# Attention pairs of the second and third batches in groups of two, and the first pass's units on four PSUM banks

## The chip, the cores and the metric

The kernel runs on one core of one Trainium2 chip. The metric is device time in microseconds of one execution. Five engines work side by side, each on its own queue, in order: PE (TensorE), DVE (VectorE), ACT (ScalarE), POOL (GpSimd) and SP, which issues the DMAs. An instruction that waits for a semaphore holds up all that stands behind it on its engine.

## What is computed

Attention over 8 batches, 8 heads, 576 positions and 64 channels, with a local mask on four heads (a window of 32) and a strided mask on the other four (every 32nd position), and then a feed-forward layer of 2048 channels on the result:

```python
def _attn_ref(q, k, v):
    scores = scale * np.matmul(q, k.transpose(0, 1, 3, 2))
    rel = pos[:, None] - pos[None, :]
    mask_local = (rel >= 0) & (rel < stride)
    mask_strided = (rel >= 0) & (pos[None, :] % stride == pos[:, None] % stride)
    ...
    attn = np.exp(scores - np.max(scores, axis=-1, keepdims=True))
    attn = attn / (np.sum(attn, axis=-1, keepdims=True) + 1e-09)
    return np.matmul(attn, v)

def _moe_ref(x, w_in, w_out):
    h = x @ w_in
    g = h * (1.0 / (1.0 + np.exp(-1.702 * h)))
    return (g @ w_out)
```

x holds the attention's result, 4608 tokens by 512 channels.

## The kernel before

**Passes and slots.** The first layer (x times w_in) is done batch by batch, in passes. Pass 0 (the first batch) is 64 plain *units* of six matmuls of 128x288 each, eight for each of the eight slices n of the weights (`unit`, `plain`). Every later pass is 56 *products* of six such matmuls, seven for each slice (`product`), whose seven results `combine` adds up on ACT and DVE. Every operand is a high and a low part; the six matmuls are high by high, high by low and low by high, over two chunks. One unit or product is one *slot* of a hand-written order: the main loop (the last lines of the listing) issues the matmuls of slot s and then, with `sided(s)`, whatever was registered for that slot with `side(s, f, ...)`, in the order of registration. All five engines keep this program order. Pass 0 runs to slot 60 (its last three units lie among the next pass's products), pass 1 is slots 61 to 116, pass 2 slots 117 to 172, and so on. Slots 0 to 7 are issued inside the opening, a list of steps written out by hand.

**Attention beside it.** While pass b runs, the attention of batch b+1 is done in its slots. A batch is six *pairs*, three local (l) and three strided (s). A pair goes through `scores` (32 or 48 small matmuls on PE), `masked` and `maxima` (DVE), `below` (POOL, subtracts the maximum), `exps` (ACT), `totals` (DVE, a sum and a reciprocal), `scaled` (POOL), `turn` (four transposes on PE, then a copy on ACT), `values` (small matmuls on PE) and copies of the result on ACT. For the batches with b above 2 pairs go in groups of two (`groups_of`): the scores of both in one run, into the two banks `s_banks` side by side, and the values of both in one run into the two banks `v_banks` (mx of the second set, mz of the first). For the pairs of batches 1 and 2, in passes 0 and 1, a pair goes alone, one each seven slots, and its values go into `s_banks`.

**Weights beside it.** In pass 0 the raw weights of slice i are made ready every seven slots: `w_scale` and `w_low` (ACT), `w_join` (DVE), `w_high` (ACT, casts and stores a plain copy), `w_low_part` (DVE). Slice i is used from unit 8i on. In pass 1 the sums of slice i, that the products need, are made from the plain copies: `t_load` (DMA), four `t_sum` (POOL, tile `sums`), `t_high` (ACT), `t_low` (DVE), at slots 49 (i=0), 59, 65, 72, 79, 86, 93 and 100 for `t_sum`; the second product of slice i needs `t_low`. Passes 2 and later have no `t_sum`.

**Banks.** `place` gives a unit of pass 0 its PSUM bank, in turn out of the six of `six`; a unit pair of the same bank is two slots apart, and `unit_out` copies the bank out (ACT, or DVE for f=1) and stores it.

Of the kernel before, what the change touches and what calls it, by code (L numbers as in the profile page):

```python
# [19 lines left out]
B, H, S, D = 8, 8, 576, 64  # L20
# [9 lines left out]
HALF = S // 2  # L30
FP = DFF // (2 * P)
PAIRS = 6
# [24 lines left out]
def _pairs():  # L57
    out = []
    for b in range(B):
        x = [[(kind, b, U * i) for i in range(PAIRS // 2)] for kind in "ls"]  # L60
        out += x[0] + x[1] if b == 0 else [u for i in range(PAIRS // 2) for u in (x[b < 3][i], x[b > 2][i])]
    return out


# [6 lines left out]
def attn_ffn(ctx, tc, qk, vs, weights, masks, ident, out):  # L71
# [44 lines left out]
    hbuf = cut(AT_H, HALF, 6)  # L116
# [45 lines left out]
    for j in (1, 2, 3, 0, 4, 5):  # L162
# [3 lines left out]
        t = prs[j].rearrange("p (i m) -> p i m", i=4)  # L166
# [174 lines left out]
    def values(p, banks, at=0):  # L341

        kind, b, c = pairs[p]
        nq = _size(kind)[0]
        v, pt = vts[p], pts[p % 2]
        n0 = QL if kind == "l" else RES[c] * NPOS
        for g in range(2):
            for w, (q0, n, _, nk) in enumerate(windows(kind)):
                if kind == "s":
                    n = min(n0, (w + 1) * WS) - w * WS  # L350
                for u in range(U):
                    i = U * g + u
                    o = g * n0 + (q0 if kind == "l" else w * WS)
                    for j in range(2):
                        slot = j ^ u
                        rows = slice(slot * D, slot * D + nk)
                        matmul(
                            banks[u][j * D : (j + 1) * D, at + o : at + o + n],
                            lhsT=v[rows, i, w, :], rhs=pt[rows, i * nq + q0 : i * nq + q0 + n],
                            start=True, stop=True,  # L360
                        )
        return lambda u, *how: moved(p, u, banks[u][:, at : at + 2 * n0], *how)

    def moves_of(moves):
        for u in range(U):
            for move in moves:
                move(u)
# [122 lines left out]
    def place(n, u):  # L490
        r, f, kh = (UNITS if n else HALVES)[u]
        j = 4 * n + 2 * r + f
        return r, f, kh, six[3 - f if j >= 4 * FP - 2 else j % 6][:, :HALF], hbuf[j % 6]

    def unit(n, u, some=(0, 1)):

# [185 lines left out]
    def side(s, f, *a):  # L682
        sides.setdefault(s, []).append((f, a))
# [19 lines left out]
    def groups_of(b, slots):  # L703

        for g in range(3):
            q, s, then = b * PAIRS + 2 * g, slots[g] + 2 * (g > 0), slots[g + 1]
            side(s, both_scores, q)
            for i in range(2):
                s += 2 * i * (g == 0)
                side(s + i, masked, q + i, s_banks, 256 * i)  # L710
                for f, d in (
                    (maxima, 0), (below, 0), (exps, 4), (totals, 5 + (i and g > 0)),
                    (scaled, 5 + (i and g > 0)),
                ):
                    side(s + d + i, f, q + i, s_banks)
                side(then - (3 - (g > 0), 1)[i], turn, q + i, s_banks[i])
            side(then, both_values, q)

    for b in range(B):
        at = first(b)  # L720
        if b == 1:
            for t, f, k in ((-11, x_sum, 1), (-10, x_sum, 3), (-9, x_sum, 2), (-6, x_high, 1),
                            (-5, x_low, 1), (-5, x_high, 4), (-4, x_low, 4), (-3, x_high, 0),
                            (-2, x_low, 0), (-1, x_high, 2), (0, x_low, 2), (1, x_sum, 4),
                            (2, x_high, 3), (3, x_low, 3), (4, x_high, 6), (5, x_low, 6),
                            (6, x_high, 5), (7, x_low, 5)):
                side(at + t, f, k, b)
        elif b:
            c = b == 2
            side(at - 10 - c, x_sum, 1, b)  # L730
            side(at - 9 - c, x_sum, 3, b)
            for k in range(7):
                t = at + 2 * k - 6 + (k == 1)
                side(t, x_high, k, b)
                side(t + 1, x_low, k, b)
            side(at - 4, x_sum, 2, b)
            side(at, x_sum, 4, b)
        if 1 < b < B - 1:
            groups_of(b + 1, [at + t for t in (3, 16, 30, 44)])
        for i in range(PAIRS if b < 2 else 0):  # L740
            p = (b + 1) * PAIRS + i
            s = at - 3 * b + 7 * i + 2 * (not b)
            t = (4, 5, 6, 11, 12) if b and not i else (5, 6, 7, 10, 12)
            side(s, scores, p, s_banks)
            side(s, load_qk, p + 2)
            for f, d in ((masked, 0), (maxima, 1), (below, 2), (exps, t[0]), (totals, t[1]), (scaled, t[2])):
                side(s + d, f, p, s_banks)
            side(s + t[3], turn, p, s_banks[0])
            side(s + t[4], lambda p=p: moves_of([values(p, s_banks)]))
            side(s + t[4], load_v, p + 2)  # L750

    def word(f, i):
        f(raws[i])
# [338 lines left out]
```

## Time and profile before

| | |
|---|---|
| median of 3 runs | 840.16 us (840.1 to 841.67) |
| profiled execution | 840.09 us, of which the span of the trace is 838.2 us |
| granted TensorE clock | 0.999 of full speed |
| PE busy | 823.9 us, 98% of the span |
| DVE, ACT, POOL busy | 538.0, 421.0, 482.5 us |
| DMA | 164.84 MB, 197 GB/s in the mean |

A row of a timeline is a start, a length, the engine, the operation, output<-input, the shape and the count; in square brackets stands the idle time ahead of it and who ended it. Almost every instruction carries line 87, that of the helper that keeps the order, so rows are told apart by tile and shape: `xa,w` with 128x288 is a unit or a product; `s<-arena 64*32` and `64*64 64x54` are scores; `s<-ident_sb` is the transposes of a turn; `arena<-arena,nmax` is `below`, `arena<-arena,rinv` is `scaled`, `sums<-sums` is `t_sum`; `raw` and `w` are the weights. Rows that follow each other with the same tiles are merged, with their count.

### The profile page before, as it was taken

To read this page: it belongs to the slowest core of one execution; us is meant where nothing else is said; L and a number is where in the kernel's file an instruction comes from. 1 tells how busy PE (TensorE), PEld (TensorE's weight loads), DVE (VectorE), ACT (ScalarE), POOL (GpSimd) and SP (SyncE) were. 2 spreads that over 40 slices of the span, in tenths; PEclk is the share of its full clock that TensorE was granted. 3 is DMA by queue.
4 is the path that set the end of the run, shared out by engine and by line. 5 is a ranking of instruction groups with operands and counts; after the bars stand their busy time and mean duration, and the time that the engine had idled before them with its cause. 6 is when DMAs were issued, how large, how long until landed. Compare 5 with 4: busy or idle time off the path is not lost. (4 is left out here: it accounts for less than half of the span.)

```text
span 838.2 us, 23960 instructions
## 1 busy us (share of the span) xinstructions
PE 823.9 (98%) x9821; PEld 800.2 (95%) x9821; DVE 538.0 (64%) x877; ACT 421.0 (50%) x660; POOL 482.5 (58%) x512
## 2 busy tenths in 40 slices
PE   7899999999999999999999999999999999999998
PEld 5799989999999999999999999999999999999997
DVE  5666777867767668677678856666555555555553
ACT  4665634434434434334346656565555555555550
POOL 4633886333442433334436269999877777777770
PEclk9999999999999999999999999999999999999999
DMA  9898775686776776857588944444443344344421
GB/s 339 302 397 325 216 230 177 190 265 208 223 242 208 238 237 187 264 205 230 187 268 255 280 147 149 128 158 145 137 141 127 127 134 144 126 127 129 143 82 51
DMA packets 112510, 164.84 MB, mean 197 GB/s; under 512 B 9744, under 2 KB 88336, under 8 KB 111504
## 3 DMA queue, kind: packets, MB, share of 16 engines
q1 hardware_dynamic: 112400, 163.31, 60.1%
q8 instruction: 77, 1.26, 0.6%
q14 instruction: 33, 0.27, 0.1%
HBM read 104.55 MB, written 58.72 MB: 195 GB/s over the span
## 5 line engine op out<-in xcount | busy, mean ns | idle before, releaser
L87 POOL TENSOR_TENSOR arena<-arena 128x256 f32<-128x256 f32 (+1 forms) x301 | 307.1, 1033 | 154.1 <-ACT arena L87 80.5
L87 DVE TENSOR_TENSOR xa<-arena,xa 128x576 fp32r<-128x576 f32 (+3 forms) x100 | 147.6, 1478 | 97.5 <-ACT xa L87 50.1
L87 PE MATMUL my<-xa,w 128*128 128x288 f32 x1128 | 179.5, 300 | 1.4 <-DVE arena L87 1.1
L87 ACT CAST xa<-arena 128x576 fp32r<-128x576 f32 (+3 forms) x103 | 115.3, 1140 | 101.8 <-PE s L87 74.1
L87 PEld LDWEIGHTS my<-xa,w 128*128 128x128 f32 x1128 | 156.3, 188 | 4.2 <-DVE arena L87 1.6
L87 ACT COPY arena<-mx 128x288 f32<-128x288 f32 (+4 forms) x181 | 62.6, 365 | 172.8 <-PE mx L87 132.2
L87 PE MATMUL mz<-xa,w 128*128 128x288 f32 x804 | 131.1, 299 | 0.8 <-POOL xa L87 0.8
L87 PE MATMUL mx<-xa,w 128*128 128x288 f32 x804 | 129.4, 298 | 0.0
L87 DVE TENSOR_TENSOR arena<-my,arena 128x288 f32<-128x288 f32 (+1 forms) x204 | 89.0, 443 | 53.0 <-PE my L87 51.0
L87 ACT ACTIVATE arena<-arena 128x1024 f32<-128x1024 f32 (+2 forms) x120 | 105.2, 877 | 23.2 <-POOL arena L87 13.6
L87 PEld LDWEIGHTS mz<-xa,w 128*128 128x128 f32 x804 | 112.8, 188 | 2.1 <-POOL xa L87 1.0
L87 PEld LDWEIGHTS mx<-xa,w 128*128 128x128 f32 x804 | 112.8, 188 | 0.8
L87 POOL TENSOR_TENSOR arena<-arena,nmax 128x432 f32<-128x432 f32 (+1 forms) x42 | 51.1, 1217 | 94.1 <-DVE nmax L87 90.8
L87 DVE TENSOR_TENSOR arena<-mz,arena 128x288 f32<-128x288 f32 (+1 forms) x166 | 70.1, 440 | 23.9 <-PE mz L87 18.5
L87 DVE TENSOR_TENSOR ga<-arena,ga 128x1792 fp32r<-128x1792 f32 (+1 forms) x25 | 51.9, 2075 | 51.8 <-ACT ga L87 28.3
L87 POOL TENSOR_TENSOR arena<-arena,rinv 96x512 f32<-96x512 f32 (+1 forms) x48 | 48.3, 1008 | 62.3 <-DVE rinv L87 53.5
L87 PE MATMUL mx<-w_out,xa 128*128 128x256 f32 x576 | 75.6, 281 | 0.0
L87 PE MATMUL mz<-w_out,xa 128*128 128x256 f32 x576 | 75.6, 281 | 0.0
L87 PE MATMUL my<-w_out,xa 128*128 128x256 f32 x576 | 75.6, 281 | 0.0
L87 PEld LDWEIGHTS mx<-w_out,xa 128*128 128x128 f32 x576 | 71.2, 188 | 0.0
L87 PEld LDWEIGHTS my<-w_out,xa 128*128 128x128 f32 x576 | 71.2, 188 | 0.0
L87 PEld LDWEIGHTS mz<-w_out,xa 128*128 128x128 f32 x576 | 71.2, 188 | 0.0
(81 smaller groups left out, 1031.8 us busy)
## 6 DMA issues: line engine op xcount, KB each, us to landing
hid<-arena SPq DMA_DIRECT2D x256, 144.0 KB, 3.2
arena<-hid SPq DMA_DIRECT2D x144, 256.0 KB, 3.2
arena<-qk SPq DMA_DIRECT2D x23, 448.0 KB, 4.8
arena<-qk SPq DMA_DIRECT2D x21, 472.0 KB, 5.7
arena<-vs SPq DMA_DIRECT2D x23, 384.0 KB, 4.3
out<-arena SPq DMA_DIRECT2D x34, 256.0 KB, 2.8
stage<-w_out SPq DMA_DIRECT2D x16, 512.0 KB, 4.2
raw<-w_in SPq DMA_DIRECT2D x7, 1024.0 KB, 9.2
```

What stands on the lines that cost most here:

```text
L87: ins = call(*args, **kw)
```

## The change

The pairs of batches 1 and 2 go through `groups_of` too. In pass 0 the three groups stand at slots 2, 20, 34 with the last values at 47; in pass 1 they stand where later passes have theirs (at+3, +16, +30, +44). The order of a batch's pairs is l, s everywhere. Units of pass 0 from slice 1 on go round four banks (the fifth and sixth of `six` for one half of the positions, the first and second for the other), and `v_banks` are the third and fourth; the last two units' banks stay as they were.

```diff
-        out += x[0] + x[1] if b == 0 else [u for i in range(PAIRS // 2) for u in (x[b < 3][i], x[b > 2][i])]
+        out += x[0] + x[1] if b == 0 else [u for i in range(PAIRS // 2) for u in (x[0][i], x[1][i])]
...
-        return r, f, kh, six[3 - f if j >= 4 * FP - 2 else j % 6][:, :HALF], hbuf[j % 6]
+        i = 3 - f if j >= 4 * FP - 2 else (j if j < 4 else (4, 5, 0, 1)[j % 4])
+        return r, f, kh, six[i][:, :HALF], hbuf[j % 6]
...
-        if 1 < b < B - 1:
-            groups_of(b + 1, [at + t for t in (3, 16, 30, 44)])
-        for i in range(PAIRS if b < 2 else 0):
-            p = (b + 1) * PAIRS + i
-            s = at - 3 * b + 7 * i + 2 * (not b)
-            t = (4, 5, 6, 11, 12) if b and not i else (5, 6, 7, 10, 12)
-            side(s, scores, p, s_banks)
-            side(s, load_qk, p + 2)
-            for f, d in ((masked, 0), (maxima, 1), (below, 2), (exps, t[0]), (totals, t[1]), (scaled, t[2])):
-                side(s + d, f, p, s_banks)
-            side(s + t[3], turn, p, s_banks[0])
-            side(s + t[4], lambda p=p: moves_of([values(p, s_banks)]))
-            side(s + t[4], load_v, p + 2)
+        if b < B - 1:
+            groups_of(b + 1, [at + t for t in (2, 20, 34, 47)] if not b else [at + t for t in (3, 16, 30, 44)])
```

What the change does to the order shows at two places. The first is in pass 0, slots 2 to 10, where the weights of slice 2 are made ready (tile `raw_371`; `w_638` before and `w_671` after is that slice's high and low parts). On DVE before, `w_join` (the one that writes `raw_371`) follows the first pair's maxima, and `w_low_part` (the last row) stands after the second pair's maxima:

```order
L87 SCALAR_TENSOR_TENSOR arena<-s_82,masks_sb 128x4x54
L87 SCALAR_TENSOR_TENSOR arena<-s_83,masks_sb 128x4x54
L87 TENSOR_REDUCE nmax_609<-arena 128x8
L87 SCALAR_TENSOR_TENSOR raw_371<-raw_371 128x1024
L87 TENSOR_REDUCE ssum_610<-arena 128x8
L87 RECIPROCAL rinv_611<-ssum_610 128x8
L87 SCALAR_TENSOR_TENSOR arena<-s_82,masks_sb 96x4x64
L87 SCALAR_TENSOR_TENSOR arena<-s_83,masks_sb 96x4x64
L87 TENSOR_REDUCE nmax_673<-arena 96x8
L87 TENSOR_TENSOR w_638<-raw_371,w_638 128x4x256
```

The same stretch of DVE after, from the second half of the first pair's mask on:

```order
L87 SCALAR_TENSOR_TENSOR arena<-s_83,masks_sb 96x4x64
L87 TENSOR_REDUCE nmax_634<-arena 96x8
L87 SCALAR_TENSOR_TENSOR arena<-s_82,masks_sb 128x4x54
L87 SCALAR_TENSOR_TENSOR arena<-s_83,masks_sb 128x4x54
L87 TENSOR_REDUCE nmax_652<-arena 128x8
L87 TENSOR_REDUCE ssum_635<-arena 96x8
L87 RECIPROCAL rinv_636<-ssum_635 96x8
L87 SCALAR_TENSOR_TENSOR raw_371<-raw_371 128x1024
L87 TENSOR_REDUCE ssum_653<-arena 128x8
L87 RECIPROCAL rinv_654<-ssum_653 128x8
L87 TENSOR_TENSOR w_671<-raw_371,w_671 128x4x256
```

Both pairs' masks, maxima and totals now stand ahead of `w_low_part`, and the first pair's totals ahead of `w_join`. ACT's rows there, after:

```order
L87 ACTIVATE raw_371<-raw_371 128x1024 x2
L87 ACTIVATE arena<-arena 96x4x128
L87 CAST w_671<-raw_371 128x4x256
L87 ACTIVATE arena<-arena 128x4x2x54
L87 COPY arena<-my_80 128x288
```

The two rows on `arena` are the two pairs' `exps`: the second is new between `w_high` (the cast) and the copy that frees bank `my_80`.

The second place is in pass 1, on POOL, around slot 79. Before, each `below` (by `nmax`) is followed by its pair's `scaled` (by `rinv`), and the four `t_sum` of a slice stand between pairs:

```order
L87 TENSOR_TENSOR sums<-sums 128x256 x4
L87 TENSOR_TENSOR arena<-arena,nmax_1623 128x4x2x54
L87 TENSOR_TENSOR arena<-arena,rinv_1625 128x4x2x54
L87 TENSOR_TENSOR sums<-sums 128x256 x4
L87 TENSOR_TENSOR arena<-arena,nmax_1751 96x4x128
L87 TENSOR_TENSOR arena<-arena,rinv_1753 96x4x128
```

After, around the same slot:

```order
L87 TENSOR_TENSOR sums<-sums 128x256 x4
L87 TENSOR_TENSOR arena<-arena,nmax_1740 96x4x128
L87 TENSOR_TENSOR sums<-sums 128x256 x4
L87 TENSOR_TENSOR arena<-arena,nmax_1759 128x4x2x54
L87 TENSOR_TENSOR arena<-arena,rinv_1742 96x4x128
L87 TENSOR_TENSOR arena<-arena,rinv_1761 128x4x2x54
```

Four `t_sum` now stand between the two `below` of a group, ahead of both `scaled`. It is so in all three groups of pass 1.

## Rows read from the trace of the kernel before

**Rows 1.** Windows: slots 8 to 60, pass 1, pass 2; start:end, length, busy us.

```profile
33.84:90.24 56.40, 55.23 (x825) 52.10 (x823) 37.92 (x61) 36.47 (x68) 23.59 (x20) 1.00 0.91 335
90.24:149.18 58.94, 57.61 (x810) 53.95 (x809) 43.38 (x79) 26.90 (x62) 41.95 (x39) 1.00 0.65 202
149.18:204.89 55.71, 55.71 (x843) 54.06 (x841) 39.49 (x82) 23.75 (x60) 21.16 (x26) 1.00 0.71 226
```

**Rows 2.** Timeline of PE: pass 0, then the same slots of pass 2.

```profile
32.33 0.69 PE L87 MATMUL s<-arena 64*64 64x54 f32 x32
...
33.84 0.95 PE L87 MATMUL my<-xa,w 128*128 128x288 f32 x6
...
39.75 0.66 PE L87 MATMUL s<-ident_sb,arena 128*128 128x128 f32 x4 [0.94 <-POOL arena L87]
...
52.05 0.74 PE L87 MATMUL s<-arena 64*32 64x64 f32 x48
...
53.60 0.95 PE L87 MATMUL my<-xa,w 128*128 128x288 f32 x6
54.39 0.95 PE L87 MATMUL mx<-xa,w 128*128 128x288 f32 x6
...
67.41 0.74 PE L87 MATMUL s<-arena 64*32 64x64 f32 x48
...
223.90 1.35 PE L87 MATMUL s<-arena 64*32 64x64 f32 x80
...
238.74 1.35 PE L87 MATMUL s<-arena 64*32 64x64 f32 x80
```

**Rows 3.** Timeline of ACT, then of DVE, around slice 2 in pass 0.

```profile
34.39 2.23 ACT L87 ACTIVATE raw<-raw 128x1024 f32<-128x1024 f32 x2
...
37.91 1.04 ACT L87 CAST w<-raw 128x1024 fp32r<-128x1024 f32 x1 [0.84 <-DVE raw L87]
38.86 0.39 ACT L87 COPY arena<-my 128x288 f32<-128x288 f32 x1
...
36.65 1.23 DVE L87 SCALAR_TENSOR_TENSOR raw<-raw 128x1024 uint32<-128x1024 uint32 x1 [2.27 <-ACT raw L87]
...
40.08 1.21 DVE L87 TENSOR_TENSOR w<-raw,w 128x1024 fp32r<-128x1024 f32 x1
```

**Rows 4.** Timeline of POOL, DVE and PE: one group of two in pass 2.

```profile
226.99 1.04 POOL L87 TENSOR_TENSOR arena<-arena,nmax 96x512 f32<-96x512 f32 x1 [5.67 <-DVE nmax L87]
...
227.83 0.60 DVE L87 TENSOR_REDUCE nmax<-arena 128x8 f32<-128x432 f32 x1
...
228.45 1.74 PE L87 MATMUL my<-xa,w 128*128 128x288 f32 x12
...
233.19 0.49 PE L87 MATMUL s<-ident_sb,arena 96*128 96x96 f32 x4
...
234.34 0.60 PE L87 MATMUL s<-ident_sb,arena 128*128 128x128 f32 x4
```

**Rows 5.** Timeline of POOL in pass 1.

```profile
96.01 5.76 POOL L87 TENSOR_TENSOR sums<-sums 128x256 f32<-128x256 f32 x4
...
112.93 4.76 POOL L87 TENSOR_TENSOR sums<-sums 128x256 f32<-128x256 f32 x4
...
120.45 1.04 POOL L87 TENSOR_TENSOR arena<-arena,rinv 96x512 f32<-96x512 f32 x1 [1.76 <-DVE rinv L87]
121.45 4.02 POOL L87 TENSOR_TENSOR sums<-sums 128x256 f32<-128x256 f32 x4
125.43 0.92 POOL L87 TENSOR_TENSOR arena<-arena,nmax 128x432 f32<-128x432 f32 x1
127.98 0.92 POOL L87 TENSOR_TENSOR arena<-arena,rinv 128x432 f32<-128x432 f32 x1 [1.63 <-ACT w L87]
```

**Rows 6.** Timeline of DVE in pass 1: two `t_low`.

```profile
121.65 1.61 DVE L87 TENSOR_TENSOR w<-sums,w 128x1024 fp32r<-128x1024 f32 x1
...
129.38 1.21 DVE L87 TENSOR_TENSOR w<-sums,w 128x1024 fp32r<-128x1024 f32 x1
```

## What the change will do to the time

> **What bounds the kernel now.** I read the busy times by stage first. PE is busy for 55.71 of 55.71 us in pass 2, for 57.61 of 58.94 in pass 1 and for 55.23 of 56.40 in slots 8 to 60 [rows 1]. So PE sets the time throughout, its clock is at full speed in all three stretches, and there are two ways to gain: less PE time for the small matmuls, and fewer waits of PE in passes 0 and 1. Passes 1 and 2 make the same comparison for us: each has 56 slots and the attention of a batch, one pair at a time in pass 1 and in groups of two in pass 2, and pass 1 takes 58.94 - 55.71 = 3.23 us longer. The PE timeline shows why. A slot alone takes 0.79 us (54.39 - 53.60). Two lone pairs and 14 slots take 15.36 us in an undisturbed stretch of pass 0 (52.05 to 67.41); a group and 14 slots take 14.84 us in pass 2 (223.90 to 238.74) [rows 2]. So a group saves about 0.52 us of PE against two lone pairs, because PE changes less often between large and small matmuls. The rest of the difference is waits such as that of 0.94 us at the first turn of pass 0, for POOL [rows 2].
>
> **What the change takes away.** Pass 1: its groups get the same slots as those of pass 2, so without new waits it takes 55.71 us: 3.23 us less. Slots 8 to 60: 53 slots at 0.79 are 41.87; a group costs PE 14.84 - 14 x 0.79 = 3.78 us (scores, two turns, values), three are 11.34; the first group's scores lie ahead of slot 8, 1.35 and 0.1 for the change to and fro, so 1.45 less. The sum is 51.76 us against 56.40: 4.64 less. Ahead of slot 8 one run of scores of 0.69 becomes one of 1.35, so slot 8 comes 0.66 later [rows 2]. Together -3.23 - 4.64 + 0.66 = -7.2 us, if nothing new is waited for. The number of instructions stays the same on every engine; only the order moves. From pass 2 on nothing changes.
>
> **What it adds in pass 0.** The first group stands in the middle of slice 2's weights. Before, ACT did `w_scale` and `w_low` from 34.39 to 36.62, DVE `w_join` to 37.88, ACT `w_high` to 38.95, and DVE `w_low_part` to 41.29 [rows 3]; unit 16, the first to use them, had 2 us to spare. Now the chain passes through both pairs' exps and totals. ACT starts 0.66 later, so `w_low` ends at 37.28. Exps and totals of one pair take 1.63 us, from the end of a `below` (125.43 + 0.92) to the start of its `scaled` (127.98), DVE and ACT free [rows 5]; some 0.2 of it is overlap and hand-over to POOL. So totals of pair 6 end at about 38.7, `w_join` (1.23) at 39.9, `w_high` (1.04) at 41.0; then exps and totals of pair 7 to 42.4, since they stand ahead of `w_low_part` on DVE, and `w_low_part` (1.21) at 43.6. PE meanwhile has slots 8 to 15 with no small work: 33.84 + 0.66 + 8 x 0.79 = 40.8, and its third matmul, the first that needs the low weights, is due 0.26 later, at 41.1. **PE waits 2.5 us** at unit 16 (2.9 with 1.63 in full, 2.0 if the hand-overs are shorter). Behind this wait stand all of PE's units; on DVE the copy that frees bank `mz` for unit 17 stands behind `w_low_part` and comes just in time. Slice 3 has seven slots between its last step and unit 24, and later slices more, so it happens once. In the last group of pass 0 the totals of the second pair stand behind `w_join` of slice 7, which waits for ACT; its turn two hand-overs later can be late by nothing or by about what the first turn is late before, 0.94 [rows 2]. I take 0.4.
>
> Four banks instead of six: a bank is used again five slots after its last matmul, 5 x 0.79 = 3.95 us, and its copy takes 0.39 [rows 3]. I cost this at nothing; the cover is that ACT and DVE come to the copy within 3.5 us. Where they don't, at unit 16, the wait is already in the 2.5. The weights' DMAs: the DMA share is 0.91 in slots 8 to 60 [rows 1], and the same bytes would have to go in some 2 us less. Loads of raw weights run slices ahead, so I cost it at nothing too, up to 1 us at the worst, the size of the largest wait seen in this pass.
>
> **What it adds in pass 1.** Take T as the start of a group's scores, 223.90 in pass 2. There `below` of the first pair starts at T + 3.09 and ends at T + 4.13, the second's maxima end at T + 4.53, and the turns come at T + 9.29 and T + 10.44 [rows 2, 4]. In pass 1 four `t_sum` stand between the two `below`. They take 4.02 to 4.76 us in rows without much DVE work, and 5.76 where DVE works on x at the start of the pass [rows 5]. For the second and third group: T + 4.13 + 4.02 (4.76), the second `below` 0.92, exps and totals 1.63, `scaled` 0.92: the second turn may start at T + 11.6 (12.4) instead of T + 10.44. That is 1.2 to 1.9 us late; I take 1.55. The first turn needs the second `below` and `scaled` of its own, 1.04: T + 10.1 to 10.9, 0.8 to 1.6 late; this is part of the same lateness, not beside it. Behind the late exps on ACT and the late totals on DVE stand `t_high` and `t_low` of the slice that is used just after the group; I add 0.15 (0 to 0.8) for its second product. So **1.7 us for each of two groups**. In the first group the two turns stand two slots apart, so its first turn decides: T + 4.13 + 4.02 to 5.76 + 0.92 + 1.04 = T + 10.1 to 11.9 against 9.29, 0.8 to 2.6 late. `t_low` of slice 1 and the low part of x for a product also stand behind the second mask on DVE. I take **2.1**, nearer to the long end because this is the place of the 5.76 row. Another wait of the same kind, `t_low` of the group's own slice behind both maxima, ends at T + 4.53 + 1.21 to 1.61 [rows 6], 5.7 to 6.1, where the product at T + 4.55 [rows 4] needs it 0.26 after its start: 0.9 to 1.3 late. It comes earlier in the same group, so PE is late once, by the larger of the two; it adds nothing.
>
> **The sum.** -7.2 + 2.5 + 0.4 + 2 x 1.7 + 2.1 = +1.2 us. On the profiled execution's 840.09 that is 841.3; the median of the runs, 840.16, is the same within 0.1.
>
> **Rivals.** A measurement of this kernel can tell about 0.2% from no change, 1.7 us.
> *Slower: `t_sum` holds the groups for longer.* It decides once the new waits exceed 7.2 + 1.7 = 8.9 us; I have 8.4. With the long rows it is 2.9 at unit 16, 1.0 at the late turn of pass 0, 1.9 + 0.8 in each of two groups and 2.6 + 0.4 in the first: 12.3 us, +5.1, 845.2; halfway, 843.2. For it speaks that a chain through four engines seldom beats the sum of its rows; against it that the 4.02 rows are as frequent as the 4.76 ones.
> *Slower: POOL and DVE hold each other up.* Of the two `t_low` rows one took 1.21 beside the `t_sum` that took 4.76, the other 1.61 in the stretch of the `t_sum` that took 4.02 [rows 5, 6]: each is long where the other is short. In a group `t_low` now starts among the `t_sum`, in each of three groups; if it lost a whole `t_sum` there, 4.76 / 4 = 1.2 us, and PE that much with it, it would be 3.6 more, 844.9. Against it stands that the two rows differ by 0.4 only. The Trainium skill, SBUF — State Buffer, section "Who interferes with whom", says that a DVE instruction with two SBUF inputs and a GpSimd instruction that reads SBUF exclude each other, and that the one that comes second is blocked until the first is done. By that rule the loss is the whole `t_sum`, 1.2; the trace agrees in sign and shows 0.4.
> *Slower: four banks are too few.* If ACT is blocked by a DMA while a copy waits, PE stands at each of some twelve turnovers of pass 0; 0.2 us each is +2.4, 843.7. Before, no wait of PE in that pass is for a bank.
> The Trainium skill, Perfetto Trace Analysis, section "Optimization Strategy", says that a gap that recurs on the engine that should be saturated can mean too few buffers; no such gap is in the trace of before, and by it this rival would show as a gap each fourth slot.
> *Faster: the short rows hold.* With 4.02 everywhere, 1.2 in two groups, 0.8 in the first and 2.0 at unit 16, the new waits are 5.2 and the time 838.1. If neither chain reached PE, which pass 2 shows for a POOL without `t_sum`, it would be 832.9. Against it stands the order on POOL: four `t_sum` of 4.02 alone are longer than the 1.2 us that the first `scaled` has to spare in pass 2.
>
> **Chances.** My forecast, within 0.2% of the time before: 0.46. Slower by the long rows: 0.25; by POOL and DVE together: 0.08; by the banks or a DMA: 0.07. Faster: 0.14. The range is 838.4 to 845.2: from just above the short rows' sum to the long rows' sum. No change is the likeliest, with its own range of 838.5 to 841.8.
>
> **What would show it.** Pass 1 should take about 61.2 us where pass 2 takes 55.71, with PE's waits at the turns, for POOL, near 1 us or more in every group, and the second `below` of each group starting right behind a `sums` row. Slots 8 to 60 should take about 54.7 us with one wait of some 2.5 us at unit 16 for DVE's `w`. Elsewhere PE's runs of 80 scores should take the 1.35 us that they take in pass 2. I am wrong if pass 1 falls to near 56, or if unit 16 does not wait; and, the other way, if gaps appear each fourth slot of pass 0.

## The result and the profile after

The changed kernel takes 848.34 us (median of 4 runs, 847.3 to 856.25) where the kernel before took 840.91 beside it: a ratio of 1.0102, 95% interval 1.0071 to 1.0134. It is slower by 1.0%. I had forecast 841.3, no difference that can be told. The profiled run took 848.76 us, its span is 847.0, 8.8 longer than before. The stages in us, from the starts of the slots' matmuls in both traces (a row ends where the next slot's first matmul starts):

| stage | before | after | difference | forecast |
|---|---|---|---|---|
| start to slot 0 | 20.67 | 22.70 | +2.03 | 0 |
| slots 0 to 7 | 13.17 | 13.25 | +0.08 | +0.66 |
| slots 8 to 60 | 56.40 | 57.63 | +1.23 | -1.74 |
| pass 1 | 58.95 | 62.42 | +3.47 | +2.27 |
| passes 2 to 6 | 279.54 | 279.44 | -0.10 | 0 |
| last pass, slots 397 to 452 | 45.31 | 47.31 | +2.00 | 0 |
| the rest, to the last matmul | 359.88 | 359.90 | +0.02 | 0 |

So the forecast is 7.5 us short: 3.0 in slots 8 to 60, 1.2 in pass 1 and 4.0 in two stretches that I had not looked at because their code is unchanged, less 0.7 in the small rows. The windows of the changed kernel, columns as in [rows 1]; the last three are a stretch inside pass 0:

```profile
35.95:93.58 57.63, 54.52 (x745) 52.06 (x743) 35.96 (x59) 35.45 (x67) 22.18 (x18) 0.97 0.90 322
93.58:156.00 62.42, 58.41 (x840) 54.65 (x841) 47.29 (x82) 26.35 (x63) 41.09 (x41) 1.00 0.61 195
156.00:211.71 55.71, 55.71 (x843) 54.05 (x841) 39.49 (x82) 23.72 (x60) 21.10 (x26) 1.00 0.72 226
40.50:44.87 4.37, 2.46 (x17) 1.99 (x15) 2.75 (x5) 3.54 (x5) 2.70 (x2) 1.00 1.07 402
44.87:48.28 3.41, 3.36 (x15) 3.34 (x16) 2.66 (x4) 1.66 (x3) 0.77 (x1) 0.50 0.96 332
48.28:52.00 3.72, 3.72 (x81) 3.56 (x82) 1.24 (x2) 3.26 (x5) 0.00 (x0) 1.00 1.04 403
```

PE no longer fills pass 1 (58.41 of 62.42), and in pass 0 there is something that [rows 1] did not have: 3.41 us at a granted clock of 0.50, the lower of the two levels (1.2 GHz). The place is unit 16, the one at which I had forecast the wait. PE there:

```profile
41.47 0.95 PE L87 MATMUL my<-xa,w 128*128 128x288 f32 x6
43.19 0.53 PE L87 MATMUL my<-xa,w 128*128 128x288 f32 x2 [0.76 <-ACT arena L87]
44.92 1.33 PE L87 MATMUL my<-xa,w 128*128 128x288 f32 x4 [1.20 <-DVE w L87]
46.05 1.64 PE L87 MATMUL mz<-xa,w 128*128 128x288 f32 x6
```

Two waits, then a unit of 1.64 us where 0.95 is normal. The first wait is for the unit's bank: ACT's copy of it stands behind `w_high` and the second pair's exps and ends at 43.14. The second, for the low weights, would have come to the same end without it. The chain behind the second wait, on DVE, ACT and POOL:

```profile
39.29 0.69 DVE L87 TENSOR_REDUCE ssum<-arena 96x8 f32<-96x520 f32 x1 [1.23 <-ACT arena L87]
...
40.13 1.17 DVE L87 SCALAR_TENSOR_TENSOR raw<-raw 128x1024 uint32<-128x1024 uint32 x1
42.89 0.61 DVE L87 TENSOR_REDUCE ssum<-arena 128x8 f32<-128x440 f32 x1 [1.58 <-ACT arena L87]
...
43.65 1.22 DVE L87 TENSOR_TENSOR w<-raw,w 128x1024 fp32r<-128x1024 f32 x1
...
41.34 1.05 ACT L87 CAST w<-raw 128x1024 fp32r<-128x1024 f32 x1 [2.08 <-DVE raw L87]
42.29 0.57 ACT L87 ACTIVATE arena<-arena 128x432 f32<-128x432 f32 x1
...
40.36 1.85 POOL L87 TENSOR_TENSOR arena<-arena,rinv 96x512 f32<-96x512 f32 x1 [1.22 <-DVE rinv L87]
43.88 1.76 POOL L87 TENSOR_TENSOR arena<-arena,rinv 128x432 f32<-128x432 f32 x1 [1.67 <-DVE rinv L87]
```

It is the chain of the prediction step by step: totals of pair 6, `w_join`, `w_high`, exps and totals of pair 7, `w_low_part`, which ends at 44.87. The next place was not in my sum: the values of slot 34, about 20 us later. First ACT, then PE:

```profile
64.79 1.05 ACT L87 CAST w<-raw 128x1024 fp32r<-128x1024 f32 x1 [3.32 <-DMA plains<-raw]
65.75 0.40 ACT L87 COPY arena<-mx 128x288 f32<-128x288 f32 x1
66.04 0.48 ACT L87 COPY arena<-s 128x384 f32<-128x384 f32 x1
66.41 1.16 ACT L87 ACTIVATE raw<-raw 128x1024 f32<-128x1024 f32 x1
67.45 0.58 ACT L87 COPY arena<-s 128x512 f32<-128x512 f32 x1
...
66.57 0.25 PE L87 MATMUL mx<-arena 64*64 64x32 f32 x2 [0.52 <-ACT arena L87]
...
68.09 0.26 PE L87 MATMUL mx<-arena 54*64 54x54 f32 x2 [0.61 <-ACT arena L87]
```

`w_high` of slice 5 writes into the buffer of a raw tile whose store (issued at 56.25, landed at 64.72) must be done. ACT stands for 3.32 us, and behind it stand the copies of both turns, which the values need. Before, the same `w_high` waited for the same store, 2.49 us, but only the copy of one lone pair's turn stood close behind it, and PE waited for nothing there:

```profile
61.66 1.05 ACT L87 CAST w<-raw 128x1024 fp32r<-128x1024 f32 x1 [2.49 <-DMA plains<-raw]
...
63.99 0.45 ACT L87 COPY arena<-s 128x384 f32<-128x384 f32 x1
```

In pass 1 the second group (T = 115.49), on PE, DVE and POOL:

```profile
115.49 1.35 PE L87 MATMUL s<-arena 64*32 64x64 f32 x80
...
121.45 1.59 PE L87 MATMUL my<-xa,w 128*128 128x288 f32 x10 [0.98 <-DVE w L87]
...
126.03 0.49 PE L87 MATMUL s<-ident_sb,arena 96*128 96x96 f32 x4
...
119.41 0.60 DVE L87 TENSOR_REDUCE nmax<-arena 128x8 f32<-128x432 f32 x1
119.93 1.46 DVE L87 TENSOR_TENSOR w<-sums,w 128x1024 fp32r<-128x1024 f32 x1
...
119.58 4.04 POOL L87 TENSOR_TENSOR sums<-sums 128x256 f32<-128x256 f32 x4
123.58 0.92 POOL L87 TENSOR_TENSOR arena<-arena,nmax 128x432 f32<-128x432 f32 x1
```

`t_low` starts at T + 4.44, behind the second maxima, and PE waits for it. The four `t_sum` stand between the two `below`, as forecast, but at the first turn (T + 10.54) PE does not wait again: it is late already.

### The profile page after: what moved, and what is told of

The parts are those of the page before. It is cut to its first block, busy times and chain, and to the rows that moved or that the text cites. A ratio compares the mean times of both kernels' runs of the same rounds, so it can differ in the third digit from the quotient of the medians.

```text
span 847.0 us, 23926 instructions
## 1 busy us (share of the span) xinstructions
PE 826.6 (98%) x9821; PEld 803.2 (95%) x9821; DVE 538.7 (64%) x877; ACT 419.5 (50%) x660; POOL 480.2 (57%) x512
## 5 line engine op out<-in xcount | busy, mean ns | idle before, releaser
L87 PE MATMUL my<-xa,w 128*128 128x288 f32 x1176 | 188.4, 301 | 7.8 <-DVE w L87 4.1
L87 PEld LDWEIGHTS my<-xa,w 128*128 128x128 f32 x1176 | 163.5, 189 | 12.3 <-DVE w L87 5.8
L87 ACT COPY arena<-mx 128x288 f32<-128x288 f32 (+4 forms) x201 | 67.3, 360 | 187.3 <-PE mx L87 139.7
L87 PE MATMUL mz<-xa,w 128*128 128x288 f32 x780 | 127.7, 300 | 0.8 <-POOL xa L87 0.7
L87 PE MATMUL mx<-xa,w 128*128 128x288 f32 x780 | 126.4, 299 | 0.4 <-DVE xa L87 0.4
L87 POOL TENSOR_TENSOR arena<-arena,nmax 96x512 f32<-96x512 f32 (+1 forms) x42 | 49.1, 1168 | 123.5 <-DVE nmax L87 119.3
L87 PEld LDWEIGHTS mz<-xa,w 128*128 128x128 f32 x780 | 110.2, 189 | 2.2 <-POOL xa L87 1.0
L87 PEld LDWEIGHTS mx<-xa,w 128*128 128x128 f32 x780 | 110.4, 189 | 1.3 <-DVE xa L87 0.6
L87 POOL TENSOR_TENSOR arena<-arena,rinv 96x512 f32<-96x512 f32 (+1 forms) x48 | 51.1, 1065 | 39.6 <-DVE rinv L87 35.1
```

The costliest lines, as they stand in the source:

```text
L87: ins = call(*args, **kw)
```

## The experiments

The table gives each kernel against the kernel before, measured beside it, and three stages of its trace in us. "Low clock" is the time from slot 8 to the last matmul at the granted clock of 0.5. The ratio is of all executions, the stages are of one: the traced executions of pass0_groups, pass1_groups and group_at_9 are 1.2 to 2.5 us quicker than their kernels' medians, and that of t_both 6.7 us.

| kernel | ratio (95%) | slots 0 to 60 | pass 1 | last pass | low clock |
|---|---|---|---|---|---|
| before, trace 1 / 2 | 1 | 69.57 / 70.55 | 58.95 / 58.99 | 45.31 / 45.79 | 0 / 0 |
| after, trace 1 / 2 | 1.0102 (1.0071 to 1.0134) | 70.88 / 74.09 | 62.42 / 65.94 | 47.31 / 47.04 | 3.4 / 10.2 |
| pass0_groups | 1.0054 (1.0036 to 1.0071) | 71.50 | 60.00 | 47.07 | 0 |
| pass1_groups | 1.0049 (1.0029 to 1.0069) | 69.51 | 62.07 | 46.52 | 0 |
| four_banks | 1.0011 (1.0001 to 1.0020) | 69.77 | 60.00 | 45.37 | 0 |
| group_at_9 | 1.0058 (1.0037 to 1.0079) | 70.29 | 61.89 | 47.43 | 0 |
| pass0_moved | 1.0098 (1.0082 to 1.0113) | 70.66 | 65.71 | 48.67 | 3.4 |
| t_low_ahead | 1.0105 (1.0072 to 1.0138) | 74.40 | 62.19 | 45.53 | 10.2 |
| t_both | 1.0102 (1.0060 to 1.0145) | 71.09 | 61.47 | 46.33 | 0 |
| all_moved | 1.0031 (1.0019 to 1.0043) | 70.34 | 61.02 | 47.66 | 0 |
| scores_apart | 1.0134 (1.0108 to 1.0159) | 69.02 | 66.59 | 46.45 | 6.8 |
| fetch_early | 1.0102 (1.0078 to 1.0126) | 68.86 | 63.98 | 45.22 | 3.4 |
| before_fetch | 0.9977 (0.9967 to 0.9986) | 71.05 | 59.03 | 45.22 | 0 |
| tuned | 0.9990 (0.9980 to 1.0001) | 70.90 | 58.48 | 46.11 | 0 |
| tuned_shifted | 1.0050 (1.0035 to 1.0066) | 72.38 | 58.10 | 45.22 | 0 |
| tuned_8 | 0.9964 (0.9953 to 0.9975) | 67.50 | 61.57 | 46.30 | 3.4 |
| tuned_pass1 | 0.9976 (0.9966 to 0.9986) | 68.89 | 59.35 | 45.23 | 0 |

### The change in parts

pass0_groups has the groups and the four banks in pass 0 alone (the cut is against the changed kernel):

```diff
-        if b < B - 1:
-            groups_of(b + 1, ...)
+        if b != 1 and b < B - 1:
+            groups_of(b + 1, ...)
+        for i in range(PAIRS if b == 1 else 0):
...
```

> Groups and four banks in pass 0 alone; pass 1 keeps its lone pairs. If the loss lies in waits inside the two passes (my theory), pass 0 carries the smaller part: slot 0 to slot 61 longer by about 2 us than before (the stretch 8 to 60 took 57.6 in the changed kernel and 56.4 before, and slot 8 comes some 0.7 later), pass 1 back at 59, about 843 us in all. The rival, that the change also lengthened the opening and the last pass by 2 us each through the loads, gives some 2 to 4 us more, 845 to 847, with slot 0 at 22.7 instead of 20.7 and the last pass at 47.3 instead of 45.3.

pass1_groups is the kernel before with groups in pass 1 alone:

```diff
-        if 1 < b < B - 1:
+        if 0 < b < B - 1:
...
-        for i in range(PAIRS if b < 2 else 0):
+        for i in range(PAIRS if b == 0 else 0):
```

> Groups in pass 1 alone; pass 0 keeps its lone pairs and its six banks. By the theory of waits pass 1 takes about 62.4 us as in the changed kernel against 58.9 before, and pass 0 its 56.4: about 844.5 us. If the waits of pass 1 were inherited from pass 0 (late t_load or late x work there), pass 1 would fall to 56 to 59 and the time to 838 to 841. If opening and last pass lengthen with this part of the change, 846.5 to 848.5.

four_banks is the kernel before with the assignment of banks of the changed one:

```diff
-        return r, f, kh, six[3 - f if j >= 4 * FP - 2 else j % 6][:, :HALF], hbuf[j % 6]
+        i = 3 - f if j >= 4 * FP - 2 else (j if j < 4 else (4, 5, 0, 1)[j % 4])
+        return r, f, kh, six[i][:, :HALF], hbuf[j % 6]
```

> The kernel before, with only the assignment of units to four PSUM banks instead of six in pass 0. By my step (four banks cost nothing) the time stays at 840.9 within 0.5 us and PE waits for no bank. By the rival of too few banks PE waits at turnovers of pass 0, 0.2 us each and some twelve of them, so +2.4, 843.3; a halved clock behind such a wait would add 1 to 2 us.

The parts add up: 0.54% and 0.49%, together the 1.02% of the whole. Neither pass gains. Both came out slower than my theory of waits inside the two passes had it (846.5 and 846.3 us where I wrote 843 and 844.5); the rival that the last pass grows too was right for both (47.07 and 46.52 us), while the opening is not late in either (slot 0 at 20.39). The banks cost 0.11%, and no unit of pass 0 waits for one: slots 8 to 60 take 56.51 us. What four_banks loses is 1.07 us at the head of pass 1 (slots 61 to 76 take 17.66 us, in the two traces of before 16.59 and 16.64). There the first load of pass 1's sums is issued 10.4 us ahead of slot 61, in the kernel before 11.8 and 11.7; but with six banks pass1_groups has it 9.8 us ahead, behind the same wait of SP for a store. pass0_groups, the other kernel with four banks and lone pairs in pass 1, takes the same 17.66 us. So I can't say that the banks cause it.

before_again and after_again repeat the two kernels for a second trace each:

> The kernel before once more, for a second trace of the same program. If the opening (slot 0 at 20.7), the step from pass 0 to pass 1 (slots 61 to 77 in 16.59) and the last pass (45.3 up to slot 453) are fixed properties of the program, they come out within 0.2 us. If they are what the DMA gave in that execution, they move by 0.5 to 2 us between two traces of one program.

> The changed kernel once more. Slot 0 at about 20.5 instead of 22.7 if the late opening was an accident of that trace; the wait at unit 16 again 0.8 + 1.2 us; a halved clock behind it perhaps, perhaps not; the wait at the values of slot 34 again between 0 and 2 us; pass 1 again 62 to 62.5; the last pass 45.5 to 47.5.

They give 842.93 and 854.1. The kernel before varies in pass 0 by 1 us, in passes 2 to 6 by 0.8 and in the last pass by 0.5. The late opening of the changed kernel was an accident of its first trace: the granted clock was at 0.50 there from 10.73 to 14.15 and from 20.97 to 24.39, in the second trace at neither place, and slot 0 is at 20.70. But behind slot 8 the half clock came again, three times, each time behind a wait of PE that the change makes: unit 16, the values of slot 34, and `t_low` in the first group of pass 1. The three stretches of the second trace:

```profile
43.66:47.07 3.41, 3.41 (x16) 3.39 (x17) 2.65 (x4) 1.63 (x4) 0.57 (x1) 0.50 0.92 297
67.55:70.96 3.41, 3.36 (x42) 3.29 (x43) 0.50 (x2) 2.31 (x8) 0.00 (x0) 0.50 0.59 168
108.51:111.92 3.41, 3.41 (x15) 3.41 (x16) 2.53 (x7) 1.91 (x3) 2.26 (x3) 0.50 0.59 168
```

What it costs can be read from kernels with the same pass 0: slots 8 to 19 took 14.22, 14.23 and 14.27 us in the three traces with the half clock (both of after, and t_low_ahead), and 12.69 and 12.70 in pass0_groups and t_both without it. So **1.5 us for one fall, and it follows the wait at unit 16 in three traces of five**. The same five traces show ACT's `w_high` waiting 3.3 to 4.4 us for the store, and slots 34 to 46 taking 15.7 to 19.4 us.

### Pass 0: moving the groups

```diff
-            groups_of(b + 1, [at + t for t in (2, 20, 34, 47)] ...)
+            groups_of(b + 1, [at + t for t in (9, 20, 34, 47)] ...)
```

> The changed kernel with the first group of pass 0 starting at slot 9 instead of slot 2, so that slice 2's weights stand ahead of it. By my theory unit 16 no longer waits (0.76 for its bank and 1.20 for the weights) and, if the halved clock of 44.87 to 48.28 comes from that wait, the clock stays full there too, 1.9 us more: 848.3 - 3.9 = 844.4. If the clock falls for another reason, only about 2 us go: 846.3. If the wait only moves to unit 24 because slice 3 meets the group there, the time stays at 848.

```diff
-            groups_of(b + 1, [at + t for t in (2, 20, 34, 47)] ...)
+            groups_of(b + 1, [at + t for t in (9, 22, 36, 49)] ...)
```

> The changed kernel with the groups of pass 0 at slots 9, 22, 36 and values to 49 instead of 2, 20, 34 and 47: slice 2's weights ahead of the first group, turns at two slots more than in the run with 9 alone, and the second group's turns at 34 and 35, behind the time at which ACT's w_high waits for a store. If unit 16's wait, the turns' waits for POOL and ACT's wait for the store are the loss of pass 0, slots 0 to 61 take 66 to 67.5 us against 70.9 in the changed kernel and 69.6 before, and the time is about 844.5. If each wait only moves to the next chain, they take 69 or more and the time stays at 847 to 848.

In group_at_9 unit 16 does not wait and the clock stays at 1.00, but the two turns of the squeezed group wait 1.49 and 1.28 us for POOL: the wait moved. In pass0_moved the waits at unit 16 and at the values are both gone, and the turns take them over: slots 0 to 60 need 70.66 us, as much as in the changed kernel. That is the poorer of the two outcomes that I had written down. Only tuned_8 (below) shows what was left: the order of two steps on ACT.

### Pass 1: t_low and t_sum

t_low_ahead moves `t_high` and `t_low` up, so that DVE does `t_low` ahead of a group's masks; t_both also moves the `t_sum` that stood between the two `below`; all_moved is t_both with the groups of pass0_moved:

```diff
+        if i % 2:
+            high, low = high - (i > 1), low - (2 if i > 1 else 1)
+        if i and i % 2 == 0:
+            sums -= 2 if i == 2 else 1
```

> The changed kernel with t_low (and t_high) of slices 3, 5 and 7 moved one or two slots up and t_low of slice 1 one slot up, so that in each group of pass 1 t_low stands ahead of both pairs' masks on DVE. If t_low alone costs PE its gaps of 1.24, 1.28 and 1.29 us, pass 1 falls from 62.4 to about 58.6 and the time from 848.3 to 844.5. By my prediction the same lateness is behind it at the turns, through the four t_sum between the two below: then the gaps move to the turns, pass 1 loses under 1.5 us and stays at 61 or more.

> As the run with t_low ahead, and t_sum of slices 2, 4 and 6 also one or two slots up, so that no t_sum stands between a group's two below. If t_low and t_sum together are the waits of pass 1, it takes 56 to 57.5 us, near pass 2's 55.7, and the time falls by some 5 to 6 us to about 843. If POOL is simply too busy in pass 1 (eight t_sum and four steps of a group in 14.8 us), the first below of each group comes late instead and pass 1 stays above 59.

> Both moves together. If they are independent, pass 0 gains some 3.5 us and pass 1 some 5.5 against the changed kernel: 839.5, a little below the kernel before. If DMA sets the end of pass 0 (the store of plains, then the load of sums, then t_sum), the gain of pass 0 is given back at the head of pass 1: 842 to 843.

With `t_low` alone the gaps for it in the second and third group are gone, and the second turns come 0.22 and 0.25 us late; slots 77 to 104 take 31.67 us instead of 33.16. So the wait was partly `t_low` and partly `t_sum`, one behind the other. (In the first group 0.58 us of the gap of 0.94 stays, and the wait for the low part of x behind it grows from 0.27 to 1.88.) With both moved, those slots take 32.45 us, but 1.40 and 1.23 us of that are something else. Against what I had written the runs fell short: t_both's pass 1 takes 61.47 us where I expected 56 to 57.5, all_moved 844.9 us in all where I expected 839.5. And t_both's median, 851.83, is no better than the changed kernel's. Its trace is its quickest execution, 845.16 at a granted clock of 1.000; the other three took 850.8 to 853.8 at 0.990 to 0.996, the level of after_again (0.994, with 10.2 us at half clock), and where it fell in them is not recorded. PE's waits in pass 1 of all_moved (us in total, times, longest):

```profile
PE s L87 <- issue: 2.0, 2, 1.3
PE my L87 <- DVE xa L87: 1.3, 1, 1.3
PE mx L87 <- DVE xa L87: 0.6, 1, 0.6
```

No wait for `w` is left, and none for POOL at a turn. The first line is a pause in the middle of a run of scores, with no releaser.

### The pauses inside the scores, and the last pass

scores_apart is all_moved with a group's scores in two slots; fetch_early also issues the fetches of the last pass two slots earlier; tuned_shifted (on tuned, below) has 100 matmuls of zeros ahead of all work:

```diff
-            side(s, both_scores, q)
+            side(slots[g], one_scores, q, 0)
+            side(slots[g] + 1, one_scores, q, 1)
```

> The kernel with both moves, and the scores of a group's second pair one slot after those of the first, so that a run has 48 and 32 matmuls instead of 80. If the pauses inside the run of 80 (0.69 and 1.27 us in pass 1, for which the trace names no releaser) are PE waiting for its instructions, which come in 16 KB packets, the slot between the two gives the packet 0.8 us and the pauses shrink to under 0.5 in sum: 1.5 us less in slots 77 to 105, against some 0.1 to 0.15 per group for the extra change between large and small matmuls, over all passes 18 groups and 2 us: about 845. If they are waits for the load of qk, they stay.

```diff
-        side(at + 3, fetch_w, h + 3)
+        side(at + 1, fetch_w, h + 3)
```

> As the run before, and in the last pass each fetch of a half of w_out's sums from the stash is issued two slots earlier. If the last pass's extra 1.2 to 2.3 us (46.5 to 47.7 against 45.3) come from those fetches landing late on ACT, it takes 45.5 or less and the time falls by 1.5 to 2 us. If another thing holds the last pass, it stays at 47.

```diff
+    for _ in range(100):
+        matmul(late[5][:, :64], lhsT=zeros[:, :P], rhs=zeros[:, :64], start=True, stop=True)
```

> The same with 100 small matmuls of zeros ahead of the first work, while PE waits for the first load. They change no result; they shift the place of all later matmuls in PE's instruction stream by some 200 instructions of the 256 that a 16 KB packet holds at 64 bytes each. In nine pauses inside score runs PE goes on 1.3 to 1.65 us after the end of such a packet. If the pauses are PE waiting for its instructions, those of pass 1 (0.9 to 1.5 us in the second and third group) vanish or move elsewhere, since the packet's edge no longer falls into the run of scores; if they belong to the data of those two groups, they stay where they are. The time should be lower than without the shift by the sum of the pauses, 1 to 2.5 us, unless they reappear at another run.

scores_apart refuted its expectation. The pauses grew to 2.38 and 2.18 us, and the edit had a fault of its own: the second scores now wait for the first pair's mask, since they share a bank, 1.4 us in each pass from 2 to 6. But it brought the values of a group and the scores of the next together, 128 small matmuls in a row, and the longer pauses fit a PE that runs out of instructions. The trace lists the packets of 16 KB that carry PE's instructions, 77 in a run; it has 19,732 matmuls and weight loads of PE in the kernel before, 256 to a packet. The pauses of pass 1 (start of the last matmul before it, packet's start and length, start of the next matmul):

```
all_moved      113.56   111.99 + 0.89   114.46
all_moved      129.40   128.56 + 0.94   130.89
t_both         115.00   113.98 + 0.96   116.40
t_both         131.34   130.08 + 0.88   132.57
scores_apart   112.15   111.92 + 1.31   114.53
scores_apart   130.97   130.61 + 0.89   133.14
```

PE goes on 1.2 to 1.65 us after the end of a packet, in these and in the pauses within a run of 80 scores of all other traces. Where two runs in succession pause, the pauses are 254 or 255 matmuls apart, each with its weight load: about two packets of 256. And the shift decides. Runs of scores on PE in tuned, then in tuned_shifted:

```profile
127.59 1.22 PE L87 MATMUL s<-arena 64*32 64x64 f32 x67
129.13 0.44 PE L87 MATMUL s<-arena 64*64 64x54 f32 x13 [0.32 <-issue]
```

```profile
58.83 0.57 PE L87 MATMUL s<-arena 64*32 64x64 f32 x35
60.74 0.34 PE L87 MATMUL s<-arena 64*32 64x64 f32 x13 [1.35 <-issue]
...
135.14 1.35 PE L87 MATMUL s<-arena 64*32 64x64 f32 x80
```

With all instructions 200 places later the pause in the third group of pass 1 is gone, and the same data bring none; so is that of pass 6, which falls from 56.65 to 55.71 us. A new one stands in pass 0 and one in pass 3. So the place follows the instruction stream, not the data. **The pauses are PE waiting for its instructions.** (The 100 matmuls themselves cost 5.8 us in the opening, where I had expected nothing: they delayed the first scores from 4.79 to 8.25, and the clock was at 0.50 from 23.31 to 30.14.) The kernel before has them too: its pass 6 shows pauses of 0.43 and 0.41 us in two runs of 80 scores, part of why that pass takes 56.69 instead of 55.7. I had read only passes 1 and 2. The Trainium skill, Runtime: NRT & Kernel Launch, section "Instruction fetch mechanics", says that instructions come in 16 KB blocks of 256 and that crossing a block is mostly hidden; the sizes agree with the trace, and "hidden" does not hold where the edge of a block falls into a run of 80 small matmuls.

The last pass is settled in one half. With earlier fetches it takes 45.22 us in fetch_early, where scores_apart took 46.45 and all_moved 47.66; so it is the fetches' landing that lengthened it. (Four of the six kernels with earlier fetches have 45.22 or 45.23; tuned and tuned_8 have 46.1 and 46.3. There ACT stands for 4.1 and 4.3 us at a copy that waits for a store of `hid`, 3.2 in before_fetch, and PE waits 0.64 and 0.85 us behind it, 9 us into the pass.) ACT's waits in the last pass before, after, and in fetch_early:

```profile
ACT w_out L87 <- DMA arena<-stash: 7.3, 5, 2.6
```

```profile
ACT w_out L87 <- DMA arena<-stash: 8.7, 4, 3.2
```

```profile
ACT w_out L87 <- DMA arena<-stash: 2.5, 4, 1.1
```

Why they land later with groups is open. In the traces of before and four_banks one of PE's instruction packets starts 16.1 to 16.2 us into the pass, ahead of the fetch that starts at 16.9; in the ten others with the old fetches and groups it comes 16.6 to 20.6 us in, mostly while a fetch runs. But t_low_ahead and the second trace of after have it at 19.0 and 19.2, as the fetch's last data packets end (19.2 in both). In the one the transfer counts as landed at 19.5 and the last pass is short (45.53), in the other at 21.3 and it is long (47.04). No run tested it.

### A version that beats both

before_fetch is the kernel before with the earlier fetches alone. tuned is all_moved with the earlier fetches, and the second mask of pass 1's first group one slot later; tuned_8 has the groups of pass 0 at (8, 21, 35, 49); tuned_pass1 has lone pairs and six banks in pass 0 and tuned's pass 1:

```diff
+                late = int(b == 2 and g == 0 and i == 1)
-                side(s + i, masked, q + i, s_banks, 256 * i)
+                side(s + i + late, masked, q + i, s_banks, 256 * i)
...
-                    (maxima, 0), (below, 0), (exps, 4), ...
+                    (maxima, late), (below, late), (exps, 4), ...
```

> The kernel before, with only the fetches from the stash issued two slots earlier in the last pass. Its two traces have a last pass of 45.3 and 45.8 us up to slot 453; if the fetches are the only thing that lengthens it, it comes out at 45.2 here, as in the run with both moves, and the time falls by 0.1 to 0.6 us, too little to tell from no change. If it falls by 2 us or more, the last pass of the kernel before was held by them too in most executions.

> Both moves, the scores of a group in one run of 80 again, the fetches two slots earlier, and in the first group of pass 1 the second pair's mask, maxima and below one slot later, behind the low part of x that PE waits for (1.32 us in the run with both moves). By the ledger so far: 844.9 with both moves, less 2.3 in the last pass, less 1.2 at the mask: 841.4, level with the kernel before or slightly ahead. If the wait at the mask only moves to the turns of that group, 842.6; if a halved clock comes with it, 844.

> As the run called tuned, with the groups of pass 0 one slot earlier (8, 21, 35 and values to 49). In that run PE still waits 4.3 us at the six turns of pass 0, 1.57 of it at one turn whose exps stand behind a w_high that waits for DVE's w_join. One slot earlier those exps stand ahead of w_high, and the third group gets the slot that it lacks against pass 2. If order alone makes these waits, 2 to 3 us of the 4.3 go and the time is about 838.5 to 839, ahead of the kernel before by 0.3%. If they come from POOL's steps taking 1.75 to 1.9 us beside DVE's work on w instead of 0.9 to 1.04, the waits stay above 3.5 us and the time at 840.5 to 841.

> The kernel before in pass 0 (lone pairs, six banks) and the tuned order of pass 1 with groups, with the earlier fetches. If the passes are independent, pass 0 takes 56.4 to 57.4 us and pass 1 57.5 to 58.5 against 59.0 with lone pairs: 840.3 less 0.5 to 1.5, so 839 to 839.8. If pass 1's gain is eaten by a pause for instructions in one of its runs of 80 scores, it is level with the kernel before with earlier fetches, 840.3.

before_fetch gains 0.23%, 1.9 us, where I had expected 0.1 to 0.6: the last pass falls to 45.22 as written, and the stretch behind it, which I had left out, to 359.13 us from 359.88 and 360.13. tuned is level with the kernel before, as written. tuned_8 is the fastest, 839.9 us (ratio 0.9964; I had written 838.5 to 839), and tuned_pass1 has 0.9976, no better than before_fetch alone. The interval of tuned_8 (0.9953 to 0.9975) overlaps that of before_fetch (0.9967 to 0.9986), so the gain over the kernel before is shown, but not that groups in passes 0 and 1 beat lone pairs with the same fetches. Waits of PE at the turns of pass 0, in tuned and in tuned_8:

```profile
PE s L87 <- POOL arena L87: 3.1, 5, 1.3
```

```profile
PE s L87 <- POOL arena L87: 0.8, 2, 0.6
```

One slot earlier, the second pair's exps stand ahead of `w_high`, which waits for DVE's `w_join`; slots 0 to 60 fall from 70.90 to 67.50 us, 1.4 to 3.5 less than in the six traces with lone pairs. So most of those waits were order. What tuned_8 still loses can be seen in its pass 1, in PE's timeline and in a window just behind:

```profile
128.18 0.44 PE L87 MATMUL s<-arena 64*64 64x54 f32 x13 [1.40 <-issue]
```

```profile
128.96:132.37 3.41, 3.41 (x17) 3.41 (x16) 3.10 (x8) 0.00 (x0) 1.50 (x2) 0.50 0.87 283
```

A pause for instructions, and 3.41 us at half clock behind it: slots 91 to 104 take 18.09 us there instead of pass 2's 14.84.

## Why the prediction was wrong, step by step

Three steps failed: the weights' DMAs at nothing, a wait of PE without a cost behind it, and "from pass 2 on nothing changes". Of the 7.5 us that the forecast is short of the trace, 1.4 are at the values of slot 34, 1.5 are half clock behind unit 16 and 2.0 are in the last pass; 1.2 are in pass 1, where terms were too small, and 2.0 in an opening that was late by accident. The small rows take back 0.7.

- **What bounds the kernel**: right. PE sets the time, and each loss is one of its waits.
- **What the change takes away** (-7.2): the size is right, where nothing is waited for. t_both's slots 77 to 104 without their two pauses take 29.8 us, pass 2's 29.7. In pass 0 the 51.76 us of the sum and the waits named below (2.4, 1.5, 1.4 and 0.3) make 57.4 of the 57.63.
- **Unit 16** (2.5): right in place, chain and size. The two gaps are 0.93 and 1.47 us, together 2.40, counted from the time at which the next matmul was due (the brackets above, 0.76 and 1.20, hold idle time only); counted from slot 8 the chain ends 8.92 us later, I had 9.1. What failed is that I ended the step there. Behind it the granted clock fell to 0.50 in three of five traces, 1.5 us each, and the sum has no term for it.
- **"The weights' DMAs ... at nothing, up to 1 us at the worst"**: this step failed. I took the DMAs for a question of bytes. The wait of `w_high` for a store was in the trace of before, 2.49 us; what the change does is to put two turns' copies behind it on ACT. It costs 1.4 us in the first trace (the values of slot 34 take 2.9 us of PE, in all_moved 1.5); of the five traces with this order the two with the half clock behind it take 18.1 and 19.4 us for slots 34 to 46, the others 15.7 to 16.6. My rival "ACT is blocked by a DMA while a copy waits" had the mechanism, but I looked for it at the banks, where but for the 0.76 us at unit 16, which the later wait there covers, nothing waits.
- **The late turn of the last group** (0.4): 0.15 and 0.13, about right. **Four banks at nothing**: right within pass 0.
- **Pass 1** (5.5): 6.7 us against pass 2, by stretch 2.9 (I had 2.1), 1.3 and 2.2 (1.7 each), and 0.4 in the last stretch. That 0.4, and another 0.4 in the 2.2, are the second `t_low` behind a group, for which I had 0.15: it takes 1.89 us. The mechanism was right, with the wait at `t_low` instead of the turn; "PE is late once, by the larger of the two" held: PE is late by 1.28 at T + 6, and the turn comes at T + 10.54 without a wait. The 2.2 also holds 0.4 of a pause for instructions, which I did not know of.
- **"From pass 2 on nothing changes"**: the code doesn't, and passes 2 to 6 agree within 0.1 us, but the last pass takes 2.0 more. It depends on a fetch that lands just in time, and [rows 1] stops at pass 2, so I could not see how thin that was.
- **The rivals.** "POOL and DVE hold each other up" was named for `t_low` and `t_sum`, and there it cost little: the `t_low` that stands among four `t_sum` of 4.04 took 1.46, 0.25 more than the 1.21 of [rows 6] and not 1.2 more; the second one, 1.89, begins at 126.24 inside a `scaled` of 0.92 that began at 126.13. It shows more elsewhere: `scaled` takes 1.85 and 1.76 us in pass 0 where it takes 1.04 and 0.92 alone, and each begins inside `w_join` or `w_low_part`. The rule of the Trainium skill that I cited (SBUF — State Buffer, "Who interferes with whom") would give 0.94 + 1.04 = 1.98 and 0.99 + 0.92 = 1.91: the trace agrees within 0.15. Since the waits at the turns went away by order alone, I had no need of it.
- **The time compared with.** I summed against a profiled execution of 840.09. Later runs of the kernel before have medians of 841.7 to 842.3, so that execution was a quick one by nearly 2 us, in pass 0 and the last pass; the range of 838.4 to 845.2 rested on its waits being typical.

The signs that I had named came out as follows: pass 1 at 62.4 where I wrote 61.2, unit 16's wait as written, no gap at each fourth slot. The waits of PE for POOL at the turns of pass 1 did not come; it waits for `w` instead, ahead of them. Slots 8 to 60 at 57.6 instead of 54.7 is where the forecast fell.

## What to carry to other kernels

Where an engine already waits for a DMA, look at what the new order puts behind that wait: the wait itself is in the old trace, and its price changes with its followers. A new wait of about 2 us on PE should be priced with its consequence, here 1.5 us of half clock more often than not, and the stretches that end "just in time" on a DMA belong in the range even where no line of them changes. Read every pass of the old trace, not two of them: the pauses for instructions were in pass 6.

## What the hardware showed that I had not expected

- **PE can run out of instructions.** Runs of 80 small matmuls, or 128 with the values directly ahead, pause for 0.3 to 2.5 us at a place that is fixed in the instruction stream (in both traces of the kernel before ahead of the same matmuls), and go on 1.2 to 1.65 us after the end of a 16 KB packet. Shifting the stream by 100 matmuls moved the pauses.
- **The granted clock falls behind a gap.** Past the opening it fell to 0.50 for 3.41 us (once 6.83) behind the two gaps at unit 16 (2.0 us idle together), behind waits of PE of 1.9 to 2.7 us idle together at the values of slot 34 and in pass 1's first group, and behind pauses of 1.6 to 2.5 us. It did not always: at unit 16 in three traces of five, and at the values in two of the four that waited 1.9 to 2.2 us there. In between PE was busy, 2.46 us of the 4.37 ahead of the fall in the first trace.
